# One block-diagonal product for the last 64 queries of two heads, with the decay added afterwards

## The chip, the cores and the metric

The kernel runs on one core of a Trainium2 chip. The metric is the device time of the whole program in microseconds (us), as a median of several runs. A profile is one execution of the program, taken by the hardware profiler; its times count from its first instruction. The engines are TensorE (PE in the profile; PEld is its loading of weights), VectorE (DVE), ScalarE (ACT), GpSimd (POOL) and SyncE (SP, which issues nearly all DMAs here). Each engine carries out its own instructions in a fixed order, and waits in that order.

## The reference

Two layers follow each other: attention with a decay, then a gated layer that mixes tokens. Batch 8, 8 heads, 576 tokens, head size 64.

```python
scores = scale * np.matmul(q, k.transpose(0, 1, 3, 2))      # scale = 1/8
cum = np.cumsum(np.log(np.clip(f, 0.0001, 1.0)), axis=-1)
scores = np.where(causal, -1000000000.0, scores + cum[:, :, :, None] - cum[:, :, None, :])
attn = softmax(scores)                                      # row maximum taken off, sum + 1e-9
x = (attn @ v) with the heads side by side                  # 8 x 576 x 512
h = np.maximum(x @ w_in, 0.0); u, v = halves of h           # 512 each
v_n = (v - mean) / sqrt(var + 1e-06)
out = (u * (w_spatial @ v_n + b_spatial)) @ w_out
```

The decay of a score is the running sum of log f at the query less that at the key. Queries 512 to 575 of a head see all 576 keys, the last 64 of them under the causal mask.

## The kernel before, in words

**Precision.** Most products run on fp32r numbers in two parts: `hi` is the cast of a value to fp32r, `lo` what the cast left over. A full product is the sum of three: hi·hi, lo·hi and hi·lo. The first pairs (`P < NQ`, that is pairs 0 to 3) use plain f32 instead.

**Tiles of attention.** The 64 heads of all batches are taken as 32 pairs. For each head of a pair, `scores(P, h)` handles queries 0 to 511 in four tiles of 128 queries (128, 256, 384, 512 keys). The 64 last queries of both heads together fill one 128-row tile, `scores_tail(P)`: rows 0 to 63 are those of head 0, rows 64 to 127 those of head 1. It works on two halves of 288 keys.

**The tables.** `prep(P, h)` builds, by DMA, the operands of one head. `ta` holds in rows 0 to 63 the high parts and in rows 64 to 127 the low parts of the queries beside a second copy of the keys' high parts, so one product of 128 rows gives hi·hi + lo·hi. `tb` holds the queries' high parts beside the keys' low parts, and in rows 64 to 67 the decay: the running sums (in two parts) beside constants -8 and 8, so that the decay comes out of the product itself. A table has 640 query columns (512, then 64 for head 0 and 64 for head 1; the other head's 64 are zero) and 576 key columns: `QK = 1216`. In the tail, the four products of a half (`ta` and `tb` of either head) accumulate in one PSUM tile; the zero columns keep the heads apart. For pairs 0 to 3 there is one f32 table `tf` of 66 rows in place of `ta` and `tb`.

**After the product**, VectorE scales, adds the mask (`zm`, bf16) and takes the row minimum of the negated scores in one instruction (L264; the tail's is L285), ScalarE takes the exponential (L266, L290), VectorE inverts the sums, GpSimd multiplies (L274, L294, L297). TensorE then transposes (L320, L333), ScalarE and VectorE split the result in two parts (L309, L310), and `attend` multiplies with v.

**Buffers.** `split(P)` loads a pair's queries and keys into `raw`, casts them to `hi` (ScalarE, L210) and subtracts for `lo` (GpSimd, L212); each of these three tiles exists once. `ta` and `tb` exist twice. `split` loads nothing for pairs 0 to 3.

**Order of the work.** Python generators write the program: `attention(b)` yields pieces of pairs, `moe(b)` those of the second layer, `load_first` those that convert weights. A number with each yield is a cost, and a loop steps whichever generator is behind by these costs. A scheduler then fixes each engine's order at compile time, by program order and by when its own simulation has the inputs ready. Where that is not wanted, `after(i, mark)` adds an edge that only orders: instruction i stands behind a marked one on its engine. In `attention`, pair P's iteration runs: `prep` of P+1, transposes of (P, 0), scores of (P+1, 0), the tail's transposes of P, `split(P + 2)`, the tail scores of P+1, attend (P, 0), transposes (P, 1), scores (P+1, 1), attend (P, 1). `w_in` and `w_out` come as 64-bit numbers; `load64` (L137 to L151) turns them into f32 with bit operations: one step on ScalarE (L141), five on VectorE, three on GpSimd and ScalarE. `load_first` does this for half of `w_in` in four chunks, beside pairs 0 to 2.

## Time and profile before

| What | us |
|---|---|
| Median of 3 runs | 814.52 |
| Lowest and highest run | 813.07, 815.46 |
| Profiled execution, first to last instruction (its span) | 811.5 |
| PE, PEld busy in it | 788.3, 704.9 |
| DVE, ACT, POOL busy in it | 567.1, 535.2, 478.1 |

No time is given for the profiled execution beside its span; the median of the runs lies 3.0 us above it. The DMA engines moved 103.5 MB. A matmul's duration in the profile reaches into the next one's, since they are pipelined; the distance from start to start is what one costs. An f32 product stands as two records. "Idle before" is the time for which an engine stood still ahead of an instruction, and the arrow names what ended the wait.

### The profile page before, as it was taken

The page shows a single profiled execution, that of the slowest core. Times are in us where ns is not written, and L with a number is a line of the kernel's source. Part 1 is how long each engine was busy: PE and PEld are TensorE (multiplying, and loading weights), DVE is VectorE, ACT ScalarE, POOL GpSimd, SP SyncE. Part 2 cuts the span into 40 slices and gives each one's busy share as a digit, 9 for nine tenths or more (in the row PEclk, how much of TensorE's full clock was granted, in tenths as well). Part 3 has the DMA queues.
Part 4 walks back from the last instruction along what each step waited for, and adds up shares of the span by engine and source line. Part 5 has one row for each costly group of instructions (what it writes and reads, how often), then busy time and mean ns, then how long its engine had stood idle before and what let it go on. Part 6 is the DMA issues. An engine that isn't in the chain of part 4 may idle for free.

```text
span 811.5 us, 15566 instructions
## 1 busy us (share of the span) xinstructions
PE 788.3 (97%) x4980; PEld 704.9 (87%) x4980; DVE 567.1 (70%) x1726; ACT 535.2 (66%) x1432; POOL 478.1 (59%) x677
## 2 busy tenths in 40 slices
PE   7999899999999999999999999999999999999997
PEld 3676678998899989998799989999899988999996
DVE  5879989676976668766776668776786658765321
ACT  5587668676776667666686667776687657764431
POOL 4767788655766647555775537566675547643151
PEclk8699999999999999999999999999999999999999
DMA  7547754456545554565554565556554664430001
GB/s 201 143 121 208 197 140 116 120 151 165 139 122 135 135 146 117 128 166 140 125 141 112 150 152 126 123 144 151 131 130 107 163 164 111 95 77 14 27 1 66
DMA packets 47476, 103.50 MB, mean 128 GB/s; under 512 B 6961, under 2 KB 15153, under 8 KB 47330
## 3 DMA queue, kind: packets, MB, share of 16 engines
q1 hardware_dynamic: 47074, 101.98, 49.8%
q8 instruction: 40, 0.66, 0.3%
q10 hardware_dynamic: 320, 0.52, 0.3%
q14 instruction: 42, 0.34, 0.1%
HBM read 39.41 MB, written 10.68 MB: 62 GB/s over the span
## 4 chain that ended last, share of the span: by engine, by line
PE 87%; DVE 5%; POOL 2%; ACT 2%; DMA 2%; issue 1%; SPq 0%; ACTq 0%; POOLq 0%; DVEq 0%
PE ps L198 47%; PE sc L198 16%; PE x L198 12%; PE tp L320 8%; PE tp L198 2%; PE tp L333 2%; DMA out_dram<-o 1%; POOL tt L274 1%; DVE w L145 1%; ACT tt L266 1%; DVE tt L264 1%; DVE eh L342 0%; DVE wa L142 0%; DVE ef L305 0%; DMA w<-in_dram 0%
## 5 line engine op out<-in xcount | busy, mean ns | idle before, releaser
L274 POOL TENSOR_SCALAR tt<-tt,sm 128x128 f32<-128x128 f32 (+3 forms) x256 | 138.3, 558 | 94.7 <-DVE sm L270 86.4
L264 DVE CUSTOM_DVE_ANT_0 tt<-sc,zm 128x128 f32<-128x128 f32 (+3 forms) x256 | 122.4, 485 | 82.4 <-PE tp L320 63.0
L309 ACT CAST eh<-tp 128x512 fp32r<-128x512 f32 (+1 forms) x270 | 111.5, 425 | 87.2 <-PE tp L320 52.5
L266 ACT ACTIVATE tt<-tt,nm 128x128 f32<-128x128 f32 (+3 forms) x256 | 144.4, 565 | 26.5 <-DVE nm L264 21.5
L310 DVE TENSOR_TENSOR el<-tp,eh 128x512 fp32r<-128x512 f32 (+1 forms) x270 | 127.9, 485 | 25.0 <-ACT eh L309 22.8
L320 PE MATMUL tp<-ident,tt 128*128 128x128 f32 x640 | 113.7, 280 | 1.3 <-DVE ef L305 0.6
L198 PE MATMUL sc<-ta 128*128 128x128 f32 (+1 forms) x336 | 107.8, 327 | 3.9 <-DVE nm L264 3.8
L198 PE MATMUL x<-eh,vt 128*128 128x320 f32 (+4 forms) x378 | 104.5, 287 | 2.7 <-POOL vt L243 1.8
L198 PE MATMUL sc<-tb 68*128 68x128 f32 (+1 forms) x336 | 104.6, 316 | 0.0
L212 POOL TENSOR_TENSOR lo<-raw,hi 128x640 fp32r<-128x640 f32 (+1 forms) x56 | 83.2, 1506 | 18.5 <-ACT hi L210 18.4
L505 POOL TENSOR_TENSOR gl<-u,gh 128x256 fp32r<-128x256 f32 x64 | 47.2, 738 | 79.3 <-ACT gh L504 76.1
L198 PE MATMUL x<-el,vt 128*128 128x256 f32 x324 | 93.4, 306 | 0.0
L320 PEld LDWEIGHTS tp<-ident,tt 128*128 128x128 f32 x640 | 76.8, 142 | 10.9 <-ACT ef L305 1.2
L198 PEld LDWEIGHTS x<-eh,vt 128*128 128x128 f32 x378 | 71.2, 189 | 5.8 <-POOL vt L243 2.7
L198 PE MATMUL ps<-sph,vnh 128*128 128x256 f32 (+1 forms) x240 | 73.3, 306 | 0.2 <-ACT o L530 0.2
L198 PE MATMUL ps<-sph,vnl 128*128 128x256 f32 (+1 forms) x240 | 71.4, 298 | 0.0
L198 PEld LDWEIGHTS sc<-ta 128*128 128x128 f32 x336 | 63.5, 189 | 9.1 <-DVE nm L264 4.9
L198 PE MATMUL ps<-spl,vnh 128*128 128x256 f32 (+1 forms) x240 | 71.2, 296 | 0.0
L198 PE MATMUL ps<-xh,winh 128*128 128x256 f32 (+1 forms) x232 | 70.1, 302 | 0.1
L198 PE MATMUL ps<-xl,winh 128*128 128x256 f32 (+1 forms) x232 | 68.9, 297 | 0.0
L368 ACT CAST xh<-x 64x256 fp32r<-64x256 f32 (+1 forms) x128 | 49.8, 392 | 28.4 <-PE x L198 26.9
L198 PE MATMUL ps<-xh,winl 128*128 128x256 f32 (+1 forms) x232 | 68.4, 295 | 0.0
(190 smaller groups left out, 2127.8 us busy)
## 6 DMA issues: line engine op xcount, KB each, us to landing
raw<-in_dram SPq DMA_DIRECT2D x28, 608.0 KB
ta<-hi SPq DMA_DIRECT2D x56, 304.0 KB
vraw<-in_dram SPq DMA_DIRECT2D x32, 320.0 KB
tb<-hi SPq DMA_DIRECT2D x56, 160.0 KB
ta<-lo SPq DMA_DIRECT2D x56, 160.0 KB
out_dram<-o SPq DMA_DIRECT2D x32, 256.0 KB
ta<-hi SPq DMA_DIRECT2D x56, 144.0 KB
tb<-lo SPq DMA_DIRECT2D x56, 144.0 KB
```

The source lines that it names most:

```text
L145: V.scalar_tensor_tensor(out=w, in0=hi, scalar=0xC0000000, in1=a, op0=ALU.bitwise_and, op1=ALU.bitwise_or)
L198: T.matmul(o, l, r, start=st, stop=sp)
L212: G.tensor_tensor(out=lo[:, c], in0=raw[:, c], in1=f32(hi[:, c]), op=ALU.subtract)
L264: V.tensor_tensor_reduce(out=t, in0=sc[:, 0:n], in1=zm[:, 640 - n:640], scale=-0.125, scalar=3.0e38, op0=ALU.add, op1=ALU.min, accum_out=n ...
L266: last["exp", P, h, i] = A.activation(t, t, AF.Exp, bias=nm[:, i:i + 1], scale=-1.0, accum_out=sm[:, i:i + 1])
L274: G.tensor_scalar(out=t, in0=t, scalar1=sm[:, i:i + 1], scalar2=1.0, op0=ALU.mult, op1=ALU.mult)
L309: A.copy(h_ap, ps)
L310: V.tensor_tensor(out=l_ap, in0=ps, in1=f32(h_ap), op=ALU.subtract)
L320: T.transpose(out=tp[:, (i - c) * 128:(i - c + 1) * 128], in_=tt[h][:, TOFF[i] + 128 * c:TOFF[i] + 128 * c + 128], identity=ident)
L333: T.transpose(out=tp[:, j * 128:(j + 1) * 128], in_=tl[:, c * 128:(c + 1) * 128], identity=ident)
L368: last[P, h] = A.copy(hi, ps[m0:m0 + 64, 0:n])
L505: G.tensor_tensor(out=gl[j][:, 0:256], in0=g[:, 0:256], in1=f32(gh[j][:, 0:256]), op=ALU.subtract)
```

## The change

1. The tail's products no longer use the tables. They take the pair's `hi` and `lo` tiles as they are: rows 0 to 63 are head 0's dimensions, rows 64 to 127 head 1's, and the 128 query columns are block-diagonal (head 0's queries are zero in head 1's rows, and the other way round). So one product of 128 rows serves both heads: hi·hi, lo·hi and hi·lo make three products for each half of the keys (one f32 product for pairs 0 to 3).
2. The decay of the tail is no longer in the product. A tile `dt` (128 x 576, f32) gets each head's running sums, 64 times over, by two DMAs from DRAM (`cum_d`, stored once at the start). GpSimd subtracts the query's sum (`cq`, made once by a transposition on TensorE and two copies on VectorE) and multiplies by -8, then adds the mask to the last 64 columns. VectorE's tail instruction adds `dt` in place of `zm`.
3. The tables lose the 128 tail columns (`QM = 1088`), the decay rows too; `prep` issues one DMA more for each head.
4. Pairs 0 to 3 now load their tail's operands into the tags of `raw`, `hi` and `lo`. `split(P + 2)` moves behind the tail scores of P+1, which read `hi` and `lo`.
5. The first ScalarE step of `w_in`'s conversion is ordered behind the exponentials of the first scores, (0, 0, 3) for the first chunk and (0, 1, 1) for the others; the loop starts the conversion's account at 0.033 in place of 0.

```diff
+QM = TL + S
@@ decay_rows
-        V.tensor_tensor_scan(out=r0[:, 0, 640:QK], data0=ones, data1=ft, ...)
-        queries_rows(r0[:], 1, V.tensor_copy, A.copy)
+        V.tensor_tensor_scan(out=r0[:, 0, TL:QM], data0=ones, data1=ft, ...)
+        V.tensor_copy(r0[:, 1, 0:TL], r0[:, 0, TL:2 * TL])
+        SY.dma_start(out=cum_d[:], in_=r0[:, 0, TL:QM])
+    def tail_sums(r0):
+        tp = PS['t'].tile([128, 512], F32, name="tp")
+        T.transpose(out=tp[:, 0:64], in_=r0[:, 0, QM - 128:QM], identity=ident[0:64, 0:64])
+        for h in range(2):
+            V.tensor_copy(cq[64 * h:64 * h + 64, :], tp[64:128, 32 * h:32 * h + 32])
@@ load64
-        A.activation(af, hi.bitcast(F32), AF.Abs)
+        after(A.activation(af, hi.bitcast(F32), AF.Abs), behind)
@@ load_first
-            load64(..., ("dma", 0, 1))
+            load64(..., ("dma", 0, 1),
+                   ("exp", 0, 0, 3) if c == 0 else ("exp", 0, 1, 1))
@@ split
         if P < NQ:
+            raw = wk.tile([128, 128 + S], F32, name="rawt", tag=("raw", "hi", "lo", "raw")[P])
+            SY.dma_start(out=raw, in_=qk[P][:, TL:QK])
+            parts[P] = (raw,)
             return
@@ prep
-        SY.dma_start(out=f32(ta[0:64, :]), in_=hi[p, :])
-        SY.dma_start(out=f32(ta[64:128, 0:640]), in_=lo[p, 0:640])
-        SY.dma_start(out=f32(ta[64:128, 640:QK]), in_=hi[p, 640:QK])
+        SY.dma_start(out=f32(ta[0:64, 0:TL]), in_=hi[p, 0:TL])
+        SY.dma_start(out=f32(ta[64:128, 0:TL]), in_=lo[p, 0:TL])
+        SY.dma_start(out=f32(ta[0:64, TL:QM]), in_=hi[p, 640:QK])
+        SY.dma_start(out=f32(ta[64:128, TL:QM]), in_=hi[p, 640:QK])
...
+    def prep_tail(P):
+        dt = wk.tile([128, S], F32, name="dt", tag="dt")
+        for h in range(2):
+            st = cum_d[32 * h + P:32 * h + P + 1, :]
+            SY.dma_start(out=dt[64 * h:64 * h + 64, :],
+                         in_=bass.AP(tensor=st.tensor, offset=st.offset, ap=[[0, 64], list(st.ap[-1])]))
+        G.tensor_scalar(out=dt, in0=dt, scalar1=cq[:, P:P + 1], scalar2=-8.0, op0=ALU.subtract, op1=ALU.mult)
+        G.tensor_tensor(out=dt[:, TL:S], in0=dt[:, TL:S], in1=zm[:, 640:704], op=ALU.add)
+        tab[P] = dt
@@ scores_tail
-            for h in range(2):
-                qkt(sc[:, 0:288], P, h, 512, k0, 288, h == 0, h == 1)
-            V.tensor_tensor_reduce(out=tl[:, k0:k0 + 288], in0=sc[:, 0:288],
-                                   in1=zm[:, 0:288] if j == 0 else zm[:, 640:928], scale=-0.125, ...)
+            ts = parts[P]
+            pr = ((ts[0], ts[0]),) if len(ts) == 1 else ((ts[0], ts[0]), (ts[1], ts[0]), (ts[0], ts[1]))
+            o = TL if len(ts) == 2 else 0
+            for n, (q, k) in enumerate(pr):
+                mm(sc[:, 0:288], q[:, o:o + 128], k[:, o + 128 + k0:o + 128 + k0 + 288], n == 0, n == len(pr) - 1)
+            V.tensor_tensor_reduce(out=tl[:, k0:k0 + 288], in0=sc[:, 0:288], in1=dt[:, k0:k0 + 288],
+                                   scale=-0.125, ...)
@@ attention
+                split(0)
+                tail_sums(r0s[0])
+                prep_tail(0)
                 warm = ps_a.tile([128, 512], F32, name="x0")
...
                 prep(P + 1, 1)
+                prep_tail(P + 1)
...
             yield from transposes_tail(P)
+            if nxt:
+                yield from scores_tail(P + 1)
             if P + 2 < NPAIR:
                 split(P + 2)
-            if nxt:
-                yield from scores_tail(P + 1)
@@ the first loop
-        da, dw = 0.0, 0.0
+        da, dw = 0.0, 0.033
```

More of the change, by code (lines that the diff above doesn't have):

```diff
@@ L61, in attn_gmlp_kernel @@
     make_identity(nc, ident)
-    zm = cst.tile([128, 928], BF16, name="zm")
+    zm = cst.tile([128, 704], BF16, name="zm")
     G.memset(zm, 0.0)
@@ L67, in attn_gmlp_kernel @@
     for p0 in (0, 64):
-        G.affine_select(out=zm[p0:p0 + 64, 864:928], in_=zm[p0:p0 + 64, 864:928], compare_op=ALU.is_ge,
+        G.affine_select(out=zm[p0:p0 + 64, 640:704], in_=zm[p0:p0 + 64, 640:704], compare_op=ALU.is_ge,
                         fill=-8.0 * BIG, base=0, pattern=[[-1, 64]], channel_multiplier=1)
@@ L73, in attn_gmlp_kernel @@
     G.memset(lnc[:, 1:2], -0.5)
-    rows_d = dr.tile([64, 4, QK], F32, name="rows_d")
+    rows_d = dr.tile([64, 4, QM], F32, name="rows_d")
     rows_v = rows_d[:].rearrange("(h n) r s -> r n h s", h=2)
+    cum_d = dr.tile([64, S], F32, name="cum_d")
+    cq = cst.tile([128, 32], F32, name="cq")
     def decay_consts(r, rows):
         r = f32(r)
-        G.memset(r[:, 0:rows, 0:640], -8.0)
-        G.memset(r[:, rows:2 * rows, 640:QK], 8.0)
-        for p0, h in ((0, 0), (32, 1)):
-            V.memset(r[p0:p0 + 32, :, S - 64 * h:640 - 64 * h], 0.0)
-    def queries_rows(r, rows, copy, copy_tail):
-        r_ = f32(r)
-        copy(r[:, rows:2 * rows, 0:TL], r_[:, 0:rows, 640:640 + TL])
-        for p0, h in ((0, 0), (32, 1)):
-            copy_tail(r[p0:p0 + 32, rows:2 * rows, TL + 64 * h:S + 64 * h], r_[p0:p0 + 32, 0:rows, 640 + TL:QK])
+        G.memset(r[:, 0:rows, 0:TL], -8.0)
+        G.memset(r[:, rows:2 * rows, TL:QM], 8.0)
     def decay_rows():
@@ L97, in decay_rows @@
         V.memset(ones, 1.0)
-        r0 = cst.tile([64, 2, QK], F32, name="r0", tag="el")
+        r0 = cst.tile([64, 2, QM], F32, name="r0", tag="el")
         decay_consts(r0[:], 1)
@@ L133, in after, with load64 @@
                 mybir.DependencyClass.NoSync, mybir.DependencyReason.DATA), reason="order")
-    def load64(src, dh, dl, raw, w, a, mark=None):
+    def load64(src, dh, dl, raw, w, a, mark=None, behind=None):
         after(SY.dma_start(out=raw, in_=src), mark)
@@ L158, in load_first @@
             t = ws.tile([128, DM], U32, name="wa")
-            load64(win_v[:, c, DM:2 * DM, :], winh[:, c, DM:2 * DM], winl[:, c, DM:2 * DM], raw, w[:], t[:], ("dma", 0, 1))
+            load64(win_v[:, c, DM:2 * DM, :], winh[:, c, DM:2 * DM], winl[:, c, DM:2 * DM], raw, w[:], t[:], ("dma", 0, 1),
+                   ("exp", 0, 0, 3) if c == 0 else ("exp", 0, 1, 1))
             yield 500
@@ L212, in split @@
             G.tensor_tensor(out=lo[:, c], in0=raw[:, c], in1=f32(hi[:, c]), op=ALU.subtract)
-        parts[P] = (f32(hi[:]), f32(lo[:]))
+        parts[P] = (hi, lo)
     def prep(P, h):
@@ L218, in prep @@
         if P < NQ:
-            ta = wk.tile([66, QK], F32, name="tf", tag="ta", bufs=2)
-            SY.dma_start(out=ta[0:64, :], in_=qk[P, p, :])
+            ta = wk.tile([66, QM], F32, name="tf", tag="ta", bufs=2)
+            SY.dma_start(out=ta[0:64, 0:TL], in_=qk[P, p, 0:TL])
+            SY.dma_start(out=ta[0:64, TL:QM], in_=qk[P, p, 640:QK])
             last['dma', P, h] = SY.dma_start(out=ta[64:66, :], in_=r0s[0][32 * h + P:32 * h + P + 1])
@@ L246, in qkt @@
     def qkt(o, P, h, q0, k0, n, first, final):
-        k0 += 640
+        k0 += TL
         ts = tab[P, h]
```

23 lines of the change are left out of this document (12 added, 11 removed).

## The prediction

> **What bounds the kernel now.** I read the page's busy table first, then the stretches by stage, then the timeline around one tail in the middle of the run, then the first 40 us instruction by instruction. The profiled span is 811.5 us; the three timed runs have a median of 814.5, so about 3 us lie around the span, and I add the change of the span to the median.
>
> ```profile
> span 811.5 us, 15566 instructions
> ...
> PE 788.3 (97%) x4980; PEld 704.9 (87%) x4980; DVE 567.1 (70%) x1726; ACT 535.2 (66%) x1432; POOL 478.1 (59%) x677
> ```
>
> ```profile
> 10.00:20.00 10.00, 7.41 (x18) 4.48 (x17) 5.88 (x19) 5.20 (x14) 1.80 (x2) 0.62 0.80 217
> 20.00:60.00 40.00, 39.38 (x158) 27.51 (x157) 31.98 (x100) 26.02 (x72) 29.09 (x34) 0.80 0.47 131
> 60.00:140.00 80.00, 72.23 (x393) 57.02 (x392) 73.96 (x217) 56.35 (x155) 64.28 (x85) 1.00 0.63 164
> 140.00:780.00 640.00, 635.14 (x4244) 589.52 (x4244) 446.45 (x1376) 436.18 (x1170) 366.53 (x526) 1.00 0.50 125
> ```
>
> The columns of the second view are TensorE, its weight loads, VectorE, ScalarE, GpSimd (busy us and count), granted clock, DMA share, GB/s. There are three kernels in one. From 140 to 780 us TensorE is busy 635 of 640 us and issues 4244 matmul records, 6.6 per us; VectorE has 30% free and GpSimd 43%. Here a matmul that disappears is time that disappears. From 60 to 140 us VectorE is the fullest (74 of 80 us) and TensorE issues only 4.9 records per us. Before 60 us nothing is full all the time, and the clock is at 0.62 and 0.80 on the mean: a start-up made of waits.
>
> **Part 1, the steady tails.** A tail from pair 4 on is, for each of two halves of 288 keys, two products (ta, tb) for each head. The second half of one such tail:
>
> ```profile
> 302.49 0.29 PE L198 MATMUL sc<-ta 128*128 128x288 f32 x1
> 302.62 0.30 PE L198 MATMUL sc<-tb 68*128 68x288 f32 x1
> 302.76 0.30 PE L198 MATMUL sc<-ta 128*128 128x288 f32 x1
> 302.89 0.29 PE L198 MATMUL sc<-tb 68*128 68x288 f32 x1
> 303.03 0.40 PE L198 MATMUL ps<-winh,xh 128*128 128x512 f32 x1
> ```
>
> ```profile
> 140.00:780.00 640.00, 22.84 (x135) 17.27 (x135) 22.95 (x52) 22.58 (x52) 27.85 (x52) 1.00 0.50 125
> ```
>
> ```profile
> L198 PE MATMUL sc<-ta 128*128 128x288 f32 x112 | 33.9, 318 | 2.0 <-DVE nm L264 2.0
> L198 PE MATMUL sc<-tb 68*128 68x288 f32 x112 | 31.7, 297 | 0.0
> ```
>
> Matmuls overlap, so the durations (318, 297 ns) count double; the price is start to start: (303.03 - 302.49)/4 = 0.135 us, and a 68-row product costs as much as a 128-row one. The change needs three products for each half (high·high, low·high, high·low) in place of four: two fewer in each of 28 pairs, 224 records become 168. The row of the stretch 140 to 780 us for the tile tl alone has 52 VectorE instructions, two a pair: 26 tails lie in the saturated stage, and 26 x 2 x 0.135 = **-7.0 us**. For the two pairs (4 and 5) in VectorE's stage I count nothing (0 to -0.5).
>
> VectorE's own tail instruction keeps its length: its second input turns from bf16 into f32, and an f32 second input beside PSUM costs the same at equal shape, 419 against 418 ns:
>
> ```profile
> L310 DVE TENSOR_TENSOR el<-tp,eh 128x256 fp32r<-128x256 f32 x81 | 33.9, 419 | 7.0 <-ACT eh L309 7.0
> L264 DVE CUSTOM_DVE_ANT_0 tt<-sc,zm 128x256 f32<-128x256 f32 x64 | 26.8, 418 | 14.9 <-PE tp L320 4.8 <-PE sc L198 4.7 <-PE x L198 4.0
> L297 POOL TENSOR_SCALAR tl<-tl,sm 128x576 f32<-128x576 f32 x32 | 24.0, 751 | 2.8 <-PE tp L320 0.4
> L509 POOL TENSOR_TENSOR gt<-u,gt 128x64 fp32r<-128x64 f32 x32 | 10.1, 325 | 1.2 <-ACT gt L508 1.2
> ```
>
> **Part 2, what the decay costs elsewhere.** Per pair GpSimd gets a 128x576 tensor_scalar and a 128x64 addition: by the last two rows 0.75 + 0.33 = 1.08 us, 34 us in all. In the saturated stage GpSimd's 43% idle time hides it. In 60 to 140 us GpSimd is at 64 of 80 and some four pairs pass: 0 if it finds the holes, 4.3 if each delays VectorE's stage. GpSimd stays the less full engine, so I take near the low end, **+0.5**. This is the place for a rule that speaks against the change. Two neighbouring rows first:
>
> ```profile
> 32.44 1.26 POOL L149 TENSOR_TENSOR w<-w,wa 128x512 f32<-128x512 f32 x1
> 32.51 1.74 DVE L145 SCALAR_TENSOR_TENSOR w<-w,wa 128x512 uint32<-128x512 uint32 x1 [1.15 <-POOL winl L151]
> 13.60 0.69 DVE L145 SCALAR_TENSOR_TENSOR w<-w,wa 128x512 uint32<-128x512 uint32 x1
> ```
>
> The same VectorE operation takes 1.74 us beside a GpSimd one and 0.69 without. The Trainium skill, "SBUF — State Buffer", section "Who interferes with whom", says why: GpSimd and a VectorE operation with two SBUF inputs lock one port pair, and the later one waits for the whole of the other; the trace agrees. By that rule every new GpSimd microsecond could stop VectorE, and the sum would be 4.3 in place of 0.5; the tail instruction itself, with one input in PSUM, is not of that kind.
>
> DMA: per pair two loads of 64 x 2304 B for the sums and two more pieces in the split of ta, but the tables shrink from 1216 to 1088 columns; bytes stay about equal and DMA is at 0.50, so 0. SyncE issues four more DMAs of 0.5 to 0.7 us in some 23 us a pair: 0.
>
> **Part 3, the cast moves behind the tail.** The tail now reads hi and lo, so the split of the pair after next must wait for the tail's last product, and everything from it on is later:
>
> ```profile
> 297.54 1.20 ACT L210 CAST hi<-raw 128x1216 fp32r<-128x1216 f32 x1
> 298.81 2.96 POOL L212 TENSOR_TENSOR lo<-raw,hi 128x640 fp32r<-128x640 f32 x2 [1.39 <-ACT hi L210]
> 303.15 2.27 POOL L274 TENSOR_SCALAR tt<-tt,sm 128x128 f32<-128x128 f32 x4
> 305.39 2.52 POOL L460 TENSOR_TENSOR vnl<-vx,vnh 128x512 fp32r<-128x512 f32 x2
> 316.29 0.22 PE L198 MATMUL sc<-ta 128*128 128x128 f32 x1
> 317.21 0.75 SPq L232 DMA_DIRECT2D tb<-rows_d  x1
> ...
> 327.24 0.30 PE L198 MATMUL sc<-tb 68*128 68x288 f32 x1
> ```
>
> Before: cast at 297.5, low parts done at 301.8, first product of that pair at 316.3. After: tail ends 303.0, cast to 304.2, low parts (3.0) to 307.2 if GpSimd is free, or to 312.0 behind the 4.8 us it has queued there. The last two issues add 1.5, by the SyncE row, and a landing about 2 us (row below: issue 7.05, use 9.61). Ready at 310.7 to 315.5, needed at 316.3. It fits, by 0.8 at worst: 0, and it is the likeliest place for a loss (rival).
>
> For pair 4 it does not fit. Its raw columns are loaded at 3 us now; afterwards the buffer holds pair 3's tail operands and frees only after tail 3:
>
> ```profile
> 3.26 0.43 SPq L207 DMA_DIRECT2D raw<-in_dram  x1
> 7.05 1.38 SPq L221 DMA_DIRECT2D tf<-r  x2
> ...
> 66.67 1.24 PE L198 MATMUL sc<-tf 66*128 66x288 f32 x4
> 76.95 0.33 PE L198 MATMUL sc<-ta 128*128 128x128 f32 x1
> ```
>
> From tail 3's end (66.67 + 1.24 = 67.9): load 608 KB, by the 512 KB that took 3.39 (next fence) 4.0; cast 1.2; low parts 3.0; issue 0.7; landing 2: 78.8 against 76.95, +1.9, up to +4 if the queues are full, near 0 where VectorE fills the hole with conversions. I take **+1.5**.
>
> **Part 4, the start.**
>
> ```profile
> 9.61 1.54 PE L198 MATMUL sc<-tf 66*128 66x128 f32 x6 [0.18 <-DMA tf<-r]
> 11.90 0.66 ACT L141 ACTIVATE wa<-w 128x512 f32<-128x512 f32 x1 [1.14 <-DMA w<-in_dram]
> 12.59 0.43 DVE L142 TENSOR_SCALAR wa<-wa 128x512 f32<-128x512 f32 x1 [5.01 <-ACT wa L141]
> 13.39 0.28 DVE L264 CUSTOM_DVE_ANT_0 tt<-sc,zm 128x128 f32<-128x128 f32 x1
> ```
>
> ```profile
> 8.48 3.39 DMA w<-in_dram
> ...
> 13.74 5.93 PE sc L198 x10
> ...
> 50.29 0.97 PE sc L198 x4
> ```
>
> ```profile
> 10.00:18.00 8.00, 4.01 (x8) 1.32 (x2) 0.53 (x1) 0.65 0.99 268
> ```
>
> The first scores are ready at 10.0, but VectorE's queue has w_in's conversion ahead of them and stands 5.0 us on a DMA. Behind the exponentials, the first score goes at about 10.1: 13.39 - 10.1 = 3.3 earlier. In the chain of waits the products of pair 0 follow (5.93 us, at half clock). An f32 tail product is 0.97/2 = 0.485 at full clock; pairs 0 to 3 lose two each. Pair 0: 2 x 0.97 at half clock = 1.9; pairs 1 and 2: 1.0 each; pair 3, in VectorE's stage, 0. Together 7.2. Against it: the conversion work that VectorE did in 10 to 18 us (4.0, last row: instructions on wa) moves to a stage where it is 80% busy (31.98 of 40), so 0.8 x 4.0 = 3.2 is paid back. Net **-4.0**, between -7.2 (all absorbed) and 0 (another wait takes the place). The new transposition of the sums, two small copies and the DMA that stores the sums run beside the 26 warm-up products: 0 (up to +0.6, one issue ahead of the rows' DMA).
>
> **Sum**: -7.0 + 0.5 + 1.5 - 4.0 = -9.0: span 802.5, median **805.5**.
>
> **Rivals.** (a) Only the products count: the start keeps its length because the sums' own chain (store, load, GpSimd) or the moved conversions hold it. For: every engine has waits there. Against: the 5 us wait of VectorE is removed outright. -7.0 + 2.0 = -5: 809.5.
> (b) The start gains more. The clock means 0.62 and 0.80 are (0.38 x 10 + 0.20 x 40) x 2 = 23.6 us at half clock, right after TensorE, whose first six records end at 9.61 + 1.54 = 11.15, stands still for some 2.6 us before the chain piece at 13.74. If that wait goes, the 5.93 us chain piece may run at full clock, 3.0 less: 802.5. The Trainium skill, "TensorE: Matmul & The Clock Gate", section "Part 1: The HAM clock gate (the "warmup" mystery)", has an idle window halve the clock, and by that rule the gate would stay open here. Against: VectorE and ScalarE pace the start, and TensorE stays half idle.
> (c) No gain: tail sums late. They are issued after the pair's last table DMA (317.21 + 0.75 = 318.0 in the fence of part 3); two issues 1.5, landing 2, GpSimd 1.1 plus up to 4.8 of queue: 322.6 to 327.4, and that pair's tail ends at 327.24 + 0.3 = 327.5. Lateness of 0.35 us in 26 pairs eats the -9: 814.5.
> (d) Slower: the late low parts of part 3. Its margin is 0.8 to 5.6 us; if GpSimd's queue takes 1.4 us more than I allowed, scores wait 0.6 us in each of 26 pairs, +15.6 - 9 = +6.6: 821. It decides from 0.35 us a pair. For: GpSimd also gets 1.08 us more. Against: moe products can stand ahead of the scores.
>
> **Chances.** Forecast 0.46, (a) 0.21, (b) 0.14, (c) 0.10, (d) 0.09. A change of 0.3% (2.4 us) is about what this kernel's measurement tells from none; 814.5 - 2.4 = 812.1. Faster: 0.46 + 0.21 + 0.14 = 0.81; same 0.10; slower 0.09. For the range, the ends of the forecast's own terms (start -7.2 to 0, pair 4 0 to 4, port 0 to 4.3) taken together reach from 800 to 813; (d) and the far side of (c) are left out.
>
> **What would show it.** Steps are right if 168 tail products of 288 columns stand there at 0.135 us start to start; if the first VectorE score is at 10 to 11 us; if GpSimd gains about 34 us; if SyncE issues pair 4's raw load near 65 us and the first ta product follows some 11 us later. I am wrong if TensorE shows new waits before the scores of each pair (d), VectorE before each tail (c), or if the first moe products start no earlier than now.

## The result, and the profile after

| | median us | lowest to highest, runs | ratio to before, 95% interval |
|---|---|---|---|
| before, beside it | 814.24 | 813.07 to 815.46, 6 | |
| after | 850.58 | 846.27 to 857.88, 6 | 1.045 [1.041, 1.049] |

The change makes the kernel 4.5% slower, 36 us, where 9 us less was forecast. In this and the next tables a median is over all executions; a ratio leaves out those over 1.5% above the fastest of their kernel.

The page of the kernel after: span, busy times, granted clock in 40 slices (one slice is 21.4 us), and its group of the new GpSimd instruction (busy us, mean ns | idle ahead of it, releaser).

```profile
span 855.8 us, 15763 instructions
...
PE 798.2 (93%) x4909; PEld 706.3 (83%) x4909; DVE 602.4 (70%) x1724; ACT 532.9 (62%) x1428; POOL 561.1 (66%) x741
...
PEclk8788999969999999999999999999999999999999
...
L250 POOL TENSOR_SCALAR dt<-dt,cq 128x576 f32<-128x576 f32 x32 | 71.1, 2221 | 43.5 <-DMA dt<-cum_d 32.7
```

TensorE has 10 us more on record with 71 records fewer, GpSimd has 83 us more, not 34, and the subtraction takes 2.22 us a pair, three times the 0.75 that I took from the multiplication of the same shape. It also stands 43.5 us, most of it on its own DMA. The DMA engines move 108.5 MB where 103.5 MB went before ("bytes stay about equal" was forecast); the variant e2 below moves as much and loses almost nothing, so this is not the loss.

Further groups of the kernel after, in the view by lines: the mask's addition, VectorE's tail instruction, the high·high product of the tail, and a small cast.

```profile
L251 POOL TENSOR_TENSOR dt<-dt,zm 128x64 f32<-128x64 f32 x32 | 10.5, 329 | 0.4
L308 DVE CUSTOM_DVE_ANT_0 tl<-sc,dt 128x288 f32<-128x288 f32 x64 | 27.9, 452 | 25.7 <-PE tp L356 17.1 <-POOL tt L293 3.3 <-POOL dt L250 2.7
L201 PE MATMUL sc<-hi 128*128 128x288 f32 x56 | 18.3, 327 | 6.6 <-DVE nm L283 6.6
L365 DVE CAST eh<-el 64x128 fp32r<-64x128 f32 x27 | 37.6, 1392 | 0.9
```

The same view of the kernel before, for two of them:

```profile
L285 DVE CUSTOM_DVE_ANT_0 tl<-sc,zm 128x288 f32<-128x288 f32 x64 | 28.3, 452 | 25.4 <-PE sc L198 13.2 <-PE tp L333 11.5
L342 DVE CAST eh<-el 64x128 fp32r<-64x128 f32 x27 | 10.1, 373 | 0.8
```

The tail's products are 3 x 56 = 168 as forecast, and VectorE's tail instruction keeps its 452 ns. VectorE waits only 2.7 us in all for `dt`. The cast of 64x128, which the change doesn't touch, goes from 0.37 to 1.39 us, 27.5 us more in 27 pairs. In the trace every one of these casts of 1 us or more lies beside GpSimd's subtraction for `lo`, which now follows the moved split, and none beside the new subtraction.

By stretches, the kernel after (columns as in the prediction's view: PE, PEld, DVE, ACT, POOL, granted clock, DMA share, GB/s):

```profile
60.00:140.00 80.00, 67.98 (x321) 50.80 (x319) 58.54 (x187) 47.90 (x132) 55.84 (x71) 0.94 0.60 157
140.00:240.00 100.00, 84.62 (x523) 76.62 (x524) 83.16 (x232) 64.99 (x179) 70.89 (x93) 0.90 0.53 140
240.00:460.00 220.00, 216.97 (x1416) 199.01 (x1415) 157.36 (x454) 147.49 (x392) 151.45 (x202) 1.00 0.47 128
460.00:780.00 320.00, 309.50 (x2056) 285.87 (x2055) 237.97 (x695) 215.72 (x588) 215.22 (x285) 0.99 0.49 130
```

The kernel before, in the second and third of these stretches:

```profile
140.00:240.00 100.00, 98.68 (x668) 91.71 (x668) 74.63 (x233) 70.88 (x191) 62.09 (x89) 1.00 0.57 141
240.00:460.00 220.00, 218.31 (x1474) 203.54 (x1473) 156.67 (x490) 153.85 (x415) 129.40 (x184) 1.00 0.55 136
```

Between 140 and 240 us TensorE stands 15.4 us, against 1.3 before, and the clock falls to 0.90 on the mean. The middle of the run, by contrast, is full in both. By 240 us TensorE is 72 + 145 records behind in the first two stretches (393 against 321 by the prediction's row, 668 against 523), some 32 us at the 6.7 records a us of the kernel before (a few of these records are products that are gone). So the loss is made of new gaps and of the halved clock behind them, most of it before 240 us, where GpSimd, at 56 of 80 and 71 of 100 us, is not full.

**An account of the span.** TensorE's span is idle time, plus time that half clock takes away, plus the rest, its work at full clock. All three follow from the page: idle is span less busy; the loss to half clock is (1 - mean granted clock) x span. The mean clocks, from the view of the cores, for before, after and six of the experiments below (e2, e7, e8, e12, e17, e18):

```profile
core 0: 811.5 us, clock 0.985
core 0: 855.8 us, clock 0.966
core 0: 812.8 us, clock 0.980
core 0: 817.1 us, clock 0.988
core 0: 808.2 us, clock 0.986
core 0: 850.9 us, clock 0.962
core 0: 825.7 us, clock 0.969
core 0: 834.2 us, clock 0.981
```

The line of busy times of the same six pages, in the same order:

```profile
PE 780.1 (96%) x4909; PEld 696.3 (86%) x4909; DVE 587.2 (72%) x1724; ACT 556.0 (68%) x1460; POOL 491.5 (60%) x709
```
```profile
PE 786.5 (96%) x4980; PEld 702.8 (86%) x4980; DVE 574.1 (70%) x1726; ACT 535.4 (66%) x1432; POOL 480.2 (59%) x677
```
```profile
PE 776.0 (96%) x4909; PEld 693.1 (86%) x4909; DVE 586.1 (73%) x1724; ACT 554.1 (69%) x1460; POOL 490.3 (61%) x709
```
```profile
PE 810.8 (95%) x4980; PEld 717.5 (84%) x4980; DVE 575.6 (68%) x1726; ACT 536.5 (63%) x1432; POOL 561.1 (66%) x771
```
```profile
PE 790.4 (96%) x4868; PEld 699.5 (85%) x4868; DVE 576.9 (70%) x1726; ACT 535.4 (65%) x1432; POOL 479.9 (58%) x677
```
```profile
PE 808.6 (97%) x5092; PEld 723.5 (87%) x5092; DVE 581.0 (70%) x1726; ACT 538.3 (65%) x1432; POOL 480.9 (58%) x677
```

| us against before | span | work at full clock | idle | lost to half clock |
|---|---|---|---|---|
| before, absolute | 811.5 | 776.1 | 23.2 | 12.2 |
| after | +44.3 | -7.0 | +34.4 | +16.9 |
| e2: subtraction on ScalarE | +1.3 | -12.3 | +9.5 | +4.1 |
| e7: before, part 5 alone | +5.6 | +0.6 | +7.4 | -2.4 |
| e8: e2 without part 5 | -3.3 | -11.4 | +9.0 | -0.9 |
| e12: before, one more GpSimd operation | +39.4 | +2.4 | +16.9 | +20.1 |
| e17: before, 112 tail products fewer | +14.2 | -11.3 | +12.1 | +13.4 |
| e18: before, 112 tail products more | +22.7 | +16.6 | +2.4 | +3.7 |

Each row is one execution. That of before is the fastest of its kernel on record and that of after the slowest of its six (spans of 844.2 to 855.8), so +44.3 stands here where the medians differ by 36; the mean clock is 0.966 to 0.971 in the six.

For after: 798.2 - 0.034 x 855.8 = 769.1, against 788.3 - 0.015 x 811.5 = 776.1. The third digit of the clock and the modelled ends of products leave some 2 to 4 us open in the column of work. The products that the change takes away, 56 at 0.135 and eight f32 ones at 0.485 by the prediction's rows, are 11.4 us. So they are indeed gone from TensorE. They did not come out of the span, and the experiments had to find what put the idle time and the half clock in.

### The profile page after: what moved, and what is told of

Its sections match the earlier page's. It is cut to its first block, busy times and chain, and to the rows that moved or that the text cites. A ratio compares the mean times of both kernels' runs of the same rounds, so it can differ in the third digit from the quotient of the medians.

```text
span 855.8 us, 15763 instructions
## 1 busy us (share of the span) xinstructions
PE 798.2 (93%) x4909; PEld 706.3 (83%) x4909; DVE 602.4 (70%) x1724; ACT 532.9 (62%) x1428; POOL 561.1 (66%) x741
## 3 DMA queue, kind: packets, MB, share of 16 engines
q1 hardware_dynamic: 57970, 106.99, 46.4%
## 4 chain that ended last, share of the span: by engine, by line
PE 62%; DVE 10%; DMA 2%; ACT 2%; POOL 2%; issue 1%; SPq 0%; ACTq 0%; POOLq 0%; DVEq 0%
PE ps L201 36%; PE sc L201 10%; PE x L201 8%; PE tp L343 5%; DVE eh L365 2%; PE tp L201 2%; DVE el L333 1%; DMA out_dram<-o 1%; PE tp L356 1%; DVE tt L283 1%; POOL tt L293 1%; DVE vx L483 1%; DVE nm L312 1%; DVE xl L392 1%; DMA vraw<-in_dram 1%
## 5 line engine op out<-in xcount | busy, mean ns | idle before, releaser
L343 PE MATMUL tp<-ident,tt 128*128 128x128 f32 x640 | 116.5, 285 | 3.7 <-DVE el L333 2.9
L250 POOL TENSOR_SCALAR dt<-dt,cq 128x576 f32<-128x576 f32 x32 | 71.1, 2221 | 43.5 <-DMA dt<-cum_d 32.7
L343 PEld LDWEIGHTS tp<-ident,tt 128*128 128x128 f32 x640 | 79.5, 145 | 18.5 <-DVE el L333 3.9
L201 PE MATMUL sc<-ta 128*128 128x128 f32 x224 | 75.5, 344 | 7.6 <-DVE nm L283 4.4
L201 PE MATMUL sc<-tb 68*128 68x128 f32 x224 | 73.1, 329 | 1.5 <-DMA tb<-lo 1.5
L392 DVE TENSOR_TENSOR xl<-x,xh 64x256 fp32r<-64x256 f32 (+1 forms) x128 | 57.3, 452 | 24.0 <-ACT xh L391 21.5
```

The costliest lines, as they stand in the source:

```text
L201: T.matmul(o, l, r, start=st, stop=sp)
L250: G.tensor_scalar(out=dt, in0=dt, scalar1=cq[:, P:P + 1], scalar2=-8.0, op0=ALU.subtract, op1=ALU.mult)
L343: T.transpose(out=tp[:, (i - c) * 128:(i - c + 1) * 128], in_=tt[h][:, TOFF[i] + 128 * c:TOFF[i] + 128 * c + 128], identity=ident)
L392: V.tensor_tensor(out=lo, in0=ps[m0:m0 + 64, 0:n], in1=f32(hi), op=ALU.subtract)
```

## The experiments

### The GpSimd subtraction taken out, moved and shortened (e1, e2, e3)

e1 is the change without this instruction: the tail's decay stays the bare running sum of the key. e2 gives it to ScalarE, with `cq` eight times as large. e3 leaves it on GpSimd and turns the order round, first times -8, then plus the column, with e2's `cq`.

```diff
 e1
-        G.tensor_scalar(out=dt, in0=dt, scalar1=cq[:, P:P + 1], scalar2=-8.0, op0=ALU.subtract, op1=ALU.mult)
 e2
+        A.activation(dt, dt, AF.Identity, bias=cq[:, P:P + 1], scale=-8.0)
 e3
+        G.tensor_scalar(out=dt, in0=dt, scalar1=-8.0, scalar2=cq[:, P:P + 1], op0=ALU.mult, op1=ALU.add)
```

> The changed kernel without GpSimd's 128x576 subtraction on dt (2.2 us each, 71 us in all); its DMAs and the mask's addition stay. Left out: the tail's decay is the raw running sum of the key, so the tail's weights are others. Theory P (the long GpSimd operation, and what it holds up on VectorE, makes the loss): 805 to 820, and VectorE's busy time back from 602 towards 570. Theory S (the loss is the split that must wait for the tail): about 845 to 850, little changed. Theory O (the loss is the order of the start, w_in behind the exponentials): 845 to 850.

> The changed kernel with the subtraction done by ScalarE (-8 x dt + 8 x cq, one activation of 128x576, about 0.78 us by the exponential of the same shape) in place of GpSimd. Theory P: 808 to 825, as ScalarE has a third of its time free. Theories S and O: 845 to 850.

> The changed kernel with GpSimd's operation in another form: times -8, then plus a column of 8 x cq, in place of minus a column, times -8. If the form makes the 2.2 us, the operation takes about 0.75 us as in the row of tl (the estimate of the prediction) and theory P gives 810 to 830; if any operation of this kind that adds a column takes 2.2 us, nothing changes: 845 to 855.

| | median us (range, runs) | ratio |
|---|---|---|
| e1 | 817.3 (813.3 to 826.9, 10) | 1.003 [1.001, 1.005] |
| e2 | 816.9 (814.7 to 821.5, 5) | 1.006 [1.004, 1.008] |
| e3 | 823.5 (819.0 to 853.9, 4) | 1.010 [1.007, 1.013] |

The groups of `dt` by line, first of e2, then of e3:

```profile
L250 ACT ACTIVATE dt<-dt,cq 128x576 f32<-128x576 f32 x32 | 24.9, 778 | 27.0 <-DMA dt<-cum_d 24.6 <-POOL tl L317 1.9 <-ACT tt L285 0.4
L251 POOL TENSOR_TENSOR dt<-dt,zm 128x64 f32<-128x64 f32 x32 | 10.8, 336 | 44.1 <-ACT dt L250 38.8 <-DMA raw<-in_dram 5.2
```
```profile
L250 POOL TENSOR_SCALAR dt<-dt,cq 128x576 f32<-128x576 f32 x32 | 24.6, 770 | 49.8 <-DMA dt<-cum_d 46.4 <-DVE w L147 2.2
```

With the instruction gone, 33 of the 36 us are gone. The same arithmetic on the same tile takes 0.77 us in e3 against 2.22: not the size but the form set the price (in after all 32 last 2.21 to 2.27 us, so it is no waiting). And what is left of the change is still no gain: e1, e2 and e3 lie 0.3 to 1% above before.

### The GpSimd operation alone, on the kernel before (e12)

Nothing of the change is in e12. It adds a GpSimd subtraction on tiles that nobody reads: 384 and 192 columns of the same form from a bf16 tile, and a memset of one column (3.1 us in all, not shown in the lines below), no DMA.

```diff
+    cq = cst.tile([128, 32], F32, name="cq")
...
+    def dt_extra(P):
+        dt = wk.tile([128, 384], F32, name="dt", tag="dt")
...
+        for c in (slice(0, 384), slice(0, 192)):
+            G.tensor_scalar(out=dt[:, c], in0=zm[:, c], scalar1=cq[:, P:P + 1], scalar2=-8.0, op0=ALU.subtract, op1=ALU.mult)
...
+                dt_extra(P + 1)
```

> The kernel before with a GpSimd subtraction in the long form added for each pair, where the changed kernel has it (384 and 192 columns, read from zm, no DMA, the result unused). By the columns' share it takes about 2.2 us a pair. Theory P (GpSimd's time itself, and VectorE locked out, is the price): 825 to 840. Rival (the operation costs only where it waits for its DMA and stands in the way, or with the moved split): 814 to 819.

Measured: 851.5 us (850.0 to 852.7, 4 runs), 1.045 [1.043, 1.047], above the 825 to 840 that were expected at most. The operation and the small cast, by line, and the operation's starts in the view of its tile (the two numbers behind the durations are first and last start):

```profile
L87 POOL TENSOR_SCALAR dt<-zm,cq 128x384 f32<-128x384 bf16 (+1 forms) x62 | 79.8, 1286 | 5.8
L351 DVE CAST eh<-el 64x128 fp32r<-64x128 f32 x27 | 10.3, 380 | 0.8
L87 POOL TENSOR_SCALAR dt<-zm,cq x62: 932/1572/1898, 9.3 to 372.7; 128x384 f32<-128x384 bf16 x31, 128x192 f32<-128x192 bf16 x31
```

Two stretches of e12, then the same of before:

```profile
240.00:373.00 133.00, 126.87 (x800) 113.44 (x799) 87.98 (x271) 84.62 (x225) 111.52 (x152) 0.97 0.51 126
373.00:780.00 407.00, 402.74 (x2701) 374.01 (x2700) 289.96 (x875) 278.45 (x751) 233.43 (x332) 1.00 0.49 123
```
```profile
240.00:373.00 133.00, 132.61 (x891) 123.55 (x890) 93.43 (x293) 92.50 (x251) 78.06 (x111) 1.00 0.54 134
373.00:780.00 407.00, 403.85 (x2688) 374.26 (x2687) 278.38 (x851) 272.80 (x728) 226.38 (x327) 1.00 0.47 117
```

e12 does not place the operation where the change has it. As nobody reads the result, nothing holds it to its pair: all 62 start by 373 us, when about half of the pairs are through, while in after the 32 start from 16 to 748 us. So it is some 5 us of GpSimd a pair in the first half and nothing in the second, and that the loss is as large as the change's is luck. What it does show: up to 373 us TensorE falls behind, and behind the last of these operations it is as busy as in before (402.7 against 403.9 of 407 us). GpSimd work that feeds nothing costs TensorE time while it stands there, with GpSimd busy 112 of 133 us. In the account TensorE's idle time and the clock hold 37 of the 39 us.

VectorE is not locked out by the operation. In e12 191 VectorE instructions start while it runs; they take 66.7 us where the shortest of their forms add up to 60.1, and those that start beside no GpSimd operation 218.4 against 204.6. In after, 150 take 56.1 us against 51.8. The cast stays at 0.38 us in e12, so the stretched casts of the kernel after are no part that the loss needs.

GpSimd works in order: its multiplications of the exponentials, low parts of v and of the second layer stand behind the new operation. How this reaches TensorE is not shown step by step: TensorE's waits in e12 end on VectorE (19.6 us, 10.3 in before), ScalarE (6.8, 2.8) and DMAs of the tables (6.2, 0.2), on GpSimd itself only 2.0 us (3.6). Beside that, the compile-time scheduler, which knows of the operation, writes another order: matching each TensorE instruction's n-th occurrence, it stands on the mean 26 places from its place before (29.5 in the kernel after, 20 in e4, 2 to 18 in the kernels without a long operation that were compared). The runs do not separate these two.

### Part 5 alone, and the change without it (e7, e4, e8)

```diff
 e7: before, with part 5
-        A.activation(af, hi.bitcast(F32), AF.Abs)
+        after(A.activation(af, hi.bitcast(F32), AF.Abs), behind)
-        da, dw = 0.0, 0.0
+        da, dw = 0.0, 0.033
 e4: after, the same lines turned back; e8: e2, the same lines turned back
```

> The kernel before with part 5 alone: w_in's conversion behind the first exponentials, account at 0.033. Theory O+ (the forecast's part 4: the first score at about 10.1 in place of 13.4, of which most lasts): 809 to 812. Rival O0 (the conversions only move, paid back before 60 us): 813 to 816. Rival O- (part 5 does harm of its own, as taking it out of the changed kernel gave back 18 us): 820 or more.

> The changed kernel with part 5 undone: w_in's conversion starts as before, no order behind the exponentials, account at 0. Theory O: the loss of the first 140 us (about 15 us) comes back, 830 to 838. Theories P and S: 848 to 855, within 5 us of the changed kernel, the first scores 2 to 3 us later.

> The kernel with ScalarE's subtraction (816.9) without part 5. Theory O+: 819 to 822, the lead of 5 us at pair 3's tail is gone. Theory O-: 800 to 812. If the 18 us of the run without part 5 came from the long GpSimd operation falling in with the conversions, and not from part 5 itself, nothing clear: 813 to 819.

| | median us (range, runs) | ratio |
|---|---|---|
| e7 | 819.2 (816.4 to 825.7, 10) | 1.006 [1.004, 1.009] |
| e4 | 832.5 (828.6 to 841.0, 4) | 1.021 [1.018, 1.024] |
| e8 | 820.0 (810.0 to 825.9, 10) | 1.001 [0.998, 1.004] |

VectorE's score instructions that start in the first 20 us (the two numbers behind the durations are first and last start), for before, after, e2 and e7:

```profile
L264 DVE CUSTOM_DVE_ANT_0 tt<-sc,zm x4: 283/484/684, 13.4 to 16.0; 128x128 f32<-128x128 f32 x1, 128x256 f32<-128x256 f32 x1, 128x384 f32<-128x384 f32 x1, 128x512 f32<-128x512 f32 x1
```
```profile
L283 DVE CUSTOM_DVE_ANT_0 tt<-sc,zm x6: 288/421/692, 11.3 to 19.9; 128x128 f32<-128x128 f32 x2, 128x256 f32<-128x256 f32 x2, 128x384 f32<-128x384 f32 x1, 128x512 f32<-128x512 f32 x1
```
```profile
L283 DVE CUSTOM_DVE_ANT_0 tt<-sc,zm x8: 285/488/692, 10.3 to 19.6; 128x128 f32<-128x128 f32 x2, 128x256 f32<-128x256 f32 x2, 128x384 f32<-128x384 f32 x2, 128x512 f32<-128x512 f32 x2
```
```profile
L265 DVE CUSTOM_DVE_ANT_0 tt<-sc,zm x8: 282/482/691, 10.0 to 17.0; 128x128 f32<-128x128 f32 x2, 128x256 f32<-128x256 f32 x2, 128x384 f32<-128x384 f32 x2, 128x512 f32<-128x512 f32 x2
```

VectorE's tail instructions, all of them, for before and e7:

```profile
L285 DVE CUSTOM_DVE_ANT_0 tl<-sc,zm x64: 427/453/459, 17.8 to 725.5; 128x288 f32<-128x288 f32 x64
```
```profile
L286 DVE CUSTOM_DVE_ANT_0 tl<-sc,zm x64: 434/454/458, 12.8 to 731.1; 128x288 f32<-128x288 f32 x64
```

Part 5 does what it says: the first score comes at 10.0 in place of 13.4, and the first tail 5 us earlier. It is not kept. In e7 the tails of pairs 0 and 1 start 5 to 6 us ahead of before, those of pairs 2 to 4 by 0.5 to 1.4 us, that of pair 5 2.7 us behind, and from pair 12 to the last all stand 5.6 us behind. The conversion is paid back in full, and more. Taken out of the long-operation kernel it helps by 18 us (e4). Out of e2 it moves nothing clear: by medians e8 is 3 us above e2, by ratios some 4 us below (the executions of e8 spread from 810 to 826 for one and the same program; the account above is of its fastest).

e4 also says that the long operation has no fixed price. It is unchanged there (2.23 us a pair, GpSimd 563 us busy), and costs 13 us by medians and 16 by ratios without part 5 (e4 against e8), but 34 and 32 with it (after against e2). It counts where it falls. By stretches, of the 38 us of idle time and half clock that after has over e2, some 27 lie between 60 and 240 us and none between 240 and 460 us, though the operation runs on at one a pair.

### The table's load, the cast, and `dt` issued early (e5, e6, e9, e10, e11)

All on e2 (e10 and e11 without part 5). e5 lets pair 4's raw columns load at the start again; e6 moves the stretched cast to ScalarE; e9 and e10 issue `dt`'s DMA and its operation one tail earlier, behind `scores_tail(P + 1)`; e11 is e10 with e3's short GpSimd form.

```diff
 e5
-            raw = wk.tile([128, 128 + S], F32, name="rawt", tag=("raw", "hi", "lo", "raw")[P])
+            raw = wk.tile([128, 128 + S], F32, name="rawt", tag=("hi", "lo", "hi", "lo")[P])
 e6
-                V.tensor_copy(ET["h"][64:128, :, S:640], f32(ET["l"][64:128, :, S:640]))
+                A.copy(ET["h"][64:128, :, S:640], f32(ET["l"][64:128, :, S:640]))
 e9, e10, e11
-                prep_tail(P + 1)
...
+                prep_tail(P + 2)
```

> The kernel with ScalarE's subtraction (median 816.9) with pairs 0 to 3 using the tags hi, lo, hi, lo for their tail's operands, so that raw is free and pair 4's queries and keys can be loaded at the start as before. Theory R (the late load of pair 4 costs the lead of the start, 5 to 6 us at its first scores): pair 4's first scores at 76 to 78 in place of 81, median 810 to 814. Rival (the hole is filled by conversions, later stages decide): 815 to 819.

> The kernel with ScalarE's subtraction (816.9) with the small cast eh<-el (64x128) done by ScalarE in place of VectorE. Theory C (since the split moved, this cast meets GpSimd's low parts, 3 us, and VectorE stands behind them: mean 0.93 us there and 0.37 in the kernel before): VectorE's busy time falls by about 25 us (its own 25, of which 15 is waiting), median 808 to 813. Rival (VectorE has a quarter of its time free, the wait costs nothing): 815 to 819.

> The kernel with ScalarE's subtraction (816.9) with the sums of pair P+2 loaded right behind the tail of P+1, some 20 us ahead of their use, in place of behind the tables of the next pair. Theory D (the rest of the missing gain lies in the queue that stands on the late DMA of dt: ScalarE 24.6 us in 22 waits, GpSimd 38.8 us behind it): these waits go, and the median falls by 4 to 9 us, to 808 to 813. Rival (the queue is idle then anyway; the gain is lost to the diffuse waits of an order that is less full): 814 to 819.

> As the run before, and without part 5. Theory D with part 5 harmful by itself (4 us in the kernel before): 803 to 809. Rival: 813 to 819.

> The same with GpSimd doing the subtraction in the short form (0.77 us) in place of ScalarE: sums early, without part 5. Theory D: the 6 us between GpSimd's short form (823) and ScalarE (817) were the wait on the DMA in GpSimd's queue, so 803 to 812. Rival (every GpSimd microsecond costs, since VectorE is locked out): 815 to 822.

| | median us | ratio |
|---|---|---|
| e5 | 821.8 | 1.009 [1.006, 1.012] |
| e6 | 819.1 | 1.006 [1.003, 1.009] |
| e9 | 831.9 | 1.020 [1.017, 1.023] |
| e10 | 826.3 | 1.013 [1.009, 1.017] |
| e11 | 831.6 | 1.021 [1.019, 1.023] |

None helps. The late load and the stretched cast are real in the trace and worth nothing in the time: in e5 the first `ta` product starts at 77.1 us, in e2 at 79.3. Early issue was meant to shorten the wait for the DMA. In e10 ScalarE's wait for it grew instead, from 28.2 us in e8:

```profile
L250 ACT ACTIVATE dt<-dt,cq 128x576 f32<-128x576 f32 x32 | 24.9, 777 | 48.7 <-DMA dt<-cum_d 48.7
```

In e11 GpSimd's wait for it is 13.8 us, against 46.4 in e3, and the kernel is slower all the same. The profile taken of e9 was of an execution of 1912 us, so nothing is read from it; one of the four executions of e10 took 1974. Why early issue does harm stays open.

### The operation a stage later, the split freed, and back in its place (e13 to e16)

All on e8. e13 leaves the DMA of `dt` where it is and emits ScalarE's operation behind the pair's scores of head 0, ordered behind an exponential of these (`("exp", P, 0, 1)`; the expectation names head 1 of the pair before). e14 puts the split ahead of the tail again and lets the tails of pairs 8 to 31 read another operand (`winh`), so that no split waits for them. e15 does both, e16 is e13 with the split ahead of the tail.

```diff
 e13
+        after(A.activation(dt, dt, AF.Identity, bias=cq[:, P:P + 1], scale=-8.0), ("exp", P, 0, 1))
 e14
+                if P >= 8:
+                    mm(sc[:, 0:288], winh[:, 0, 0:128], winh[:, 1, k0:k0 + 288], n == 0, n == len(pr) - 1)
+                    continue
 e14, e15, e16
+            if P + 2 < NPAIR:
+                split(P + 2)
             if nxt:
                 yield from scores_tail(P + 1)
```

> The kernel of e8 (subtraction of the tail's decay on ScalarE, conversion early) with that ScalarE operation emitted after the pair's first scores and ordered behind the exponentials of head 1's first tiles of the pair before it, while its DMA stays where it was. Theory W (the operation stands in ScalarE's queue before its DMA has landed, some 1 us in each of 22 pairs, and the gain of the products goes there): 804 to 811, and ScalarE's wait on the DMA of dt gone from the rows. Theory S or the products' hidden: 814 to 822, with the wait gone all the same.

> The kernel of e8 with the split into high and low parts back at its old place, and the tail products of pairs 8 to 31 made from one operand that is already there (winh) in one product instead of three, so that no split waits for a tail nor a tail for a split from pair 8 on. It leaves out the tail's true products in those pairs, 2 of 3 of them as well: by the 0.135 us of a product and some 24 pairs x 3.3 it takes some 10 us more off PE. Theory S (the split is late and holds the next pair): 795 to 808. Theory that PE's products are hidden in the steady pairs: 812 to 820, although PE does less.

> The edits of e13 and e14 together; the same products are left out as in e14. If W and S each take a part of the gain: 10 us or more under e8. If neither: within 3 us of e8 (812 to 820).

> The kernel of e13 with the split emitted ahead of the tail again, as before the change; all products are made. Theory S by order alone: 804 to 811. If the split's place does not matter: as e13, within 2 us.

| | median us | ratio |
|---|---|---|
| e13 | 817.5 | 1.004 [1.002, 1.006] |
| e14 | 818.2 | 1.004 [1.002, 1.005] |
| e15 | 822.3 | 1.009 [1.008, 1.011] |
| e16 | 817.2 | 1.004 [1.002, 1.005] |

One correction to the expectations of e14 and e15: the kernel as run makes all three products of a half, each from `winh`, so it takes no work off TensorE, and their 10 us do not apply. They break the dependence between split and tail, and nothing else. In e13 the wait on the DMA is gone:

```profile
L254 ACT ACTIVATE dt<-dt,cq 128x576 f32<-128x576 f32 x32 | 24.5, 767 | 0.3 <-DMA dt<-cum_d 0.3
```

28 us of ScalarE's waits went (28.2 in e8), and the time did not move. The split's place and its dependence are worth nothing either. As causes of the missing gain both fall.

### Tail products taken away and added on the kernel before (e17, e18)

```diff
 e17: qkt, the second product (tb) of the tails of pairs 4 to 31 left out
+        ts = ts[0:1] if q0 == 512 else ts
 e18: the same product made twice
+            if q0 == 512 and t is ts[-1] and len(ts) == 2:
+                mm(o, t[0:r, q0:q0 + 128], t[0:r, k0:k0 + n], False, False)
```

> The kernel before, with the second product (operand tb) of every tail left out in pairs 4 to 31: 112 products of 288 columns fewer, 112 x 0.135 = 15.1 us less on PE, nothing else touched (it leaves out the low-part and decay terms of the tail's scores). Theory that PE sets the steady pairs, which the prediction's first term stood on: 798 to 802. Theory that the steady pairs are set by the chain through the engines beside PE: 811 to 815.

> The kernel before, with the second product of every tail in pairs 4 to 31 made twice: 112 products of 288 columns more, 15.1 us more on PE, nothing else touched (the tail's scores get that term twice). PE sets the steady pairs: 826 to 831. PE's products lie beside the other engines' chain: 814 to 818.

| | median us (range, runs) | ratio |
|---|---|---|
| e17 | 826.4 (822.2 to 828.2, 4) | 1.013 [1.009, 1.016] |
| e18 | 837.1 (836.1 to 837.7, 4) | 1.027 [1.026, 1.029] |

Both theories fail on e17: taking 15.1 us off TensorE makes the kernel 11.6 us slower. Adding 15.1 costs 22. The scheduler moves a TensorE instruction by 5.8 and 6.4 places on the mean, about alike in the two. By the account, the work is near that in both (-11.3 and +16.6). With fewer products TensorE idles 12.1 us more and loses 13.4 to half clock; 16 of these lie between 140 and 780 us, in the stage that the prediction called saturated. The trace shows one such place, a stretch of e17 and the one behind it:

```profile
102.10:105.50 3.40, 0.36 (x2) 0.00 (x0) 1.11 (x3) 1.65 (x4) 0.86 (x1) 1.00 0.52 148
105.50:112.30 6.80, 6.26 (x17) 4.95 (x18) 6.60 (x20) 5.20 (x15) 2.59 (x4) 0.50 0.13 40
```

The kernel after has the same, at 172.6 us, with GpSimd busy for the whole of it:

```profile
172.60:176.00 3.40, 0.63 (x6) 0.39 (x4) 3.24 (x6) 1.98 (x5) 3.40 (x5) 1.00 0.00 0
176.00:182.80 6.80, 5.27 (x23) 5.18 (x24) 6.71 (x15) 4.04 (x9) 3.83 (x4) 0.50 0.38 94
```

And the kernel before comes close, but keeps its clock:

```profile
128.50:131.90 3.40, 1.85 (x15) 1.65 (x14) 3.31 (x11) 2.62 (x8) 2.62 (x5) 1.00 0.93 192
131.90:135.30 3.40, 3.12 (x19) 2.79 (x19) 2.71 (x9) 3.09 (x8) 2.93 (x6) 1.00 0.21 81
```

A gap of TensorE is paid twice: once as it stands, and once in the 3.4 to 10.2 us at half clock behind it. From 36.3 us on, the trace of the kernel before has no halved stretch until its last 0.4 us; every other kernel whose profile is read here has between two and eight of them. That trace is of the fastest execution; the mean clock of the others goes down to 0.980, so some of them probably have one or two. By its verdict nothing that was run beats the kernel before; the nearest is e8, at 1.001 [0.998, 1.004] over six executions, with a median over all ten that is 5 us above it and one execution, of 810.0 us, below all of before.

One rival stays: every variant here also gets a new order (2 to 30 places on the mean), and the order of the kernel before may be a lucky one that any other loses to. Then e17 would pay for its order and not for its missing products. No run changes the order alone.

## Why the prediction was wrong, step by step

**"Here a matmul that disappears is time that disappears."** This is the step that failed for the part that was to bring the gain. The row behind it (635 of 640 us busy) is right, and so are the size and number of the products: 168 stand there, and TensorE's full-clock work falls by 7.0 us in after and by 11 to 12 in e2 and e8, where 11.4 was to go. But busy is not the same as setting the time. e17 shows it on the kernel before: less work became idle time, and idle time became half clock (whether for want of work ahead or by the new order, it does not tell). In e2 the -12.3 of work met +9.5 of idle and +4.1 of half clock. e18 shows the other direction: more work costs at least its full price. I had asked which engine is full and not what would feed it sooner.

**Part 2, GpSimd +0.5.** Two errors, and they make the loss. The price was mis-sized: 2.22 us, not 0.75, taken from a row of the same shape but of two multiplications. And the cover failed: "GpSimd's 43% idle time hides it" took a share for a place in the queue. e1 gets 33 us back by leaving the operation out and e2 34 by moving it; e12 shows that GpSimd work that nobody waits for still costs. My upper bound of 4.3 us, for 60 to 140 us alone, was too small and looked at too short a stretch: after has 17 us of idle time and half clock there and 26 in the next 100 us, e2 has 9 and 7. Only between 240 and 460 us did the idle time hide the operation, as forecast (TensorE 217.0 of 220 us busy). The rule of the port pair, weighed there from the Trainium skill, "SBUF — State Buffer", "Who interferes with whom", is not what makes the loss: VectorE's instructions beside the new operation keep their length, 56.1 us against 51.8 in after. The 64x128 cast that went from 0.37 to 1.39 us stands beside the low parts instead; it takes 0.93 in e2, which has no long operation and almost no loss.

**Part 3, the cast behind the tail: 0, and +1.5 for pair 4.** The first half held: with the split back (e16 against e13, e14 against e8) nothing moves. For pair 4 the size held without the long operation: in e2 SyncE issues the raw load at 64.7 us (forecast: near 65) and the first `ta` product starts at 79.3, 2.3 us later than before, where +1.9 was worked out. In after the load goes at 70.9 us, and the first `ta` product follows 21 us later, not 11, at 92.1 against 77.0 before:

```profile
70.89 0.34 SPq L213 DMA_DIRECT2D raw<-in_dram  x1
```
```profile
L201 PE MATMUL sc<-ta x224: 218/336/793, 92.1 to 772.6; 128*128 128x128 f32 x56, 128*128 128x384 f32 x56
```

Yet e5, which loads early and has its first `ta` product back at 77.1, gained nothing in the end: a delay at this place is not one of the span.

**Part 4, the start: -4.0.** The mechanism was right at the start and wrong behind it. The first score came at 10.3 (e2) and 11.3 (after; the forecast was 10.1). In after one VectorE instruction ahead of it, the clip of f, which the change doesn't touch, took 1.5 us longer:

```profile
3.63 2.29 DVE L95 TENSOR_SCALAR ft<-ft 64x576 f32<-64x576 f32 x1 [2.19 <-DMA ft<-in_dram]
```

The same row of the kernel before:

```profile
3.51 0.81 DVE L100 TENSOR_SCALAR ft<-ft 64x576 f32<-64x576 f32 x1 [2.07 <-DMA ft<-in_dram]
```

Why it took longer is open: GpSimd fills rows at that time in both kernels, and in e2, whose program is the same up to there, the clip takes 0.61 us. The step that failed is "0.8 x 4.0 = 3.2 is paid back". e7 paid back all it had gained by pair 5, and 5.6 us more by pair 12.

**The rivals.** (d) had the sign and the engine, GpSimd's queue, but its mechanism, low parts made late by the moved split, is not what keeps the gain away (e14, e16, both without the long operation). (c) saw that `dt` would come late on its DMA; the waits are there, and e13 shows that they cost nothing. (b) was right about the first 40 us, where the mean clock goes from 0.70 to 0.79 in after and 0.87 in e7, but behind 40 us the change opened gaps that closed it again. No rival asked what the new gaps do to the clock after the start.

**The range.** Its upper end does not follow from its terms: -7.0 with 0 at the start, 4.0 for pair 4 and 4.3 for the port is +1.3, 815.8 and not 813. The measured 850.6 lies far outside both.

What stays open: in after, and in e12 up to 373 us, how much of the new idle time comes from GpSimd's queue itself and how much from the order that the scheduler writes around a long GpSimd operation. No run held the order fixed. Open too is why part 5 makes the operation dearer (e4).

## What to carry to other kernels

A busy share near 99% says that an engine is fed well now, not that its work sets the time: ask what each following instruction will wait for once there is less of it, and test it by taking work away from the old kernel alone (e17). An operation on an engine with 40% free time is not free if the engine works in order and others wait for what stands behind it; add it alone to the old kernel before building on it, and look in the trace where it stands: an operation that nobody reads may be moved far ahead (e12). Price an operation by a row with the same operations in the same order, not by its shape.
